# Attention plus MLP on one core: later planned DMA landings, packed output passes, sums by DMA

## The chip, the cores and the metric

One core of one Trainium2 chip runs the whole kernel. The metric is the device time of one execution in microseconds, the median of several runs. TensorE is called PE, VectorE DVE, ScalarE ACT, GpSimd POOL, and SyncE SP; SP here only issues DMAs.

## What is computed

The input x is 2048 tokens by 512 channels in bf16. It is normalised once; the result feeds attention with 32 heads of 16 channels and, normalised a second time, an MLP of width 1792. The output is x + attention + MLP.

```python
xn = layernorm(x)
q, k, v = split(xn @ wqkv)                     # 32 heads of 16
a = softmax(q @ k.T * 16 ** -0.5) @ v          # per head, 2048 x 2048 scores
h = gelu(layernorm(xn) @ w1 + b1)
out = x + a @ wo + h @ w2 + b2
```

## The kernel before

**Tiling.** The queries come in four query blocks of 512 tokens; in each, the 32 heads come in eight sets of four. A set of one block is the unit of the order: 32 sets, numbered g, `NS` = 8 per block. A set runs over 16 key tiles of 128 keys. For one key tile the four heads' scores are four matmuls, each on 32 rows of the array at its own row position (helper `qk`, L1033): 128 keys by 512 queries in a PSUM bank. Each such bank is a *unit*; 2048 units in all.

**Two ways to exponentiate.** A unit goes either to ACT, which takes two or three units in one instruction (L1216) and writes bf16 weights, or to DVE. On DVE a whole key tile of four units is made: each unit is evicted with a bias into int16 bits that read as float16 are a rough exponential (`build_dve`, L1305), and further terms come from adding constants to these integers (`dve_terms`): three terms by DVE in scratch buffers (L1327), the fourth by a DMA issued from POOL that adds a constant block `sdram` in place (L1339). Each term is multiplied with v separately, so a tile on DVE costs PE five passes where one on ACT costs one (helper `pv`, L1051; four matmuls of 32 columns a pass). PE accumulates one set's products in one PSUM bank, v's extra column of ones giving the softmax's sums. At most seven of 16 tiles of a set may go to DVE (`KD`); `next_d` starts one when fewer than `OPEN` are open, fewer than `OUT` are unfinished, an int16 buffer is free, and, within the running set, at least `RES` units are left. What DVE doesn't take goes to ACT.

**After a set** (`build_opost`): DVE copies the bank to `osb` (L1368). SP sends the four rows of sums to DRAM (L1370) and fetches them back as 128 by 16 values `lc` (L1372); DVE takes reciprocals (L1375); SP writes these out (L1377) and reads them back broadcast over partitions, `rlb` (L1380); DVE multiplies (L1382) into a slot of `ont`. POOL checks with four small instructions that the sums lie in the range for which the rough exponential holds (L1389 to L1395) and collects the answer; were it false, a slow version (`_general`) would run at the end. The last set does this with DVE transposes and no DRAM (`build_opost_last`).

**Output and MLP.** Once per block, `build_out` multiplies the eight sets with rows of wo that are padded to 32 rows a head with zeros (`wo_pad`), eight passes of four matmuls (helper `mm`, L597) per tile of 128 tokens. `build_mlp` and `build_down` do the MLP of a block: w1 is loaded in pieces through SP, the Gelu is two long ACT instructions (L1499). x plus b2 is made on POOL (L1515) from a loaded `x_r`, and DVE adds the MLP's product to it in `acc` (L1523), then the output product (L1545). `build_final` does the last two sets' part.

**The order.** `_Plan` lays out all instructions before the program is built. It is a list scheduler with the engines PE, ACT, DVE, POOL, SP and ACT's queue; each step has a duration, dependencies, a priority, and `lat`, the time after its end until a DMA's data is taken to have landed (for the accumulating DMA `SHL` = 6.0; for the four DMAs after a set 1.8, 2.4, 1.8 and 4.6). Each engine then executes its instructions strictly in the order that the plan found; semaphores make it wait where the data comes later than planned. Where the plan leaves PE idle while a set is open, it puts in matmuls on zeros (`fill`, L1622).

Of the kernel before, what the change touches and what calls it, by code (L numbers as in the profile page):

```python
# [22 lines left out]
P = 128  # L23
# [456 lines left out]
def kernel(  # L480
# [38 lines left out]
    NPU, NI, NTB, NON, NW1 = 15, 8, 4, 11, 4  # L519
# [5 lines left out]
    sdram = drp.tile([P, HS * QW], I16, name="sdram")  # L525
# [9 lines left out]
    b2_sb = const.tile([P, D], BF, name="b2_sb")  # L535
# [11 lines left out]
    wo_pad = const.tile([P, NB, 2, D], BF, name="wo_pad")  # L547
# [9 lines left out]
    x_r = const.tile([P, 2, D], BF, name="x_r")  # L557
# [14 lines left out]
    lc = const.tile([P, 2, LCW], F32, name="lc")  # L572
    rc = const.tile([P, 2, LCW], F32, name="rc")
    okt = const.tile([P, 2, LCW], F32, name="okt")
    okall = const.tile([P, LCW], F32, name="okall")
    ont = const.tile([P, NON, QW], BF, name="ont")
    ot = const.tile([P, 2, D], BF, name="ot")
# [26 lines left out]
    def pen(n):  # L604
        return 0.205 * n + 0.01
# [7 lines left out]
    def act(cols):  # L613
        return cols * 0.833e-3 + 0.07
# [26 lines left out]
    SHL = 6.0  # L641
    SLOT = 1.0
    PEND = _Op()
    OUT, OPEN, RES, RESL, SLK, ALP = 4, 2, 36, 28, 55.0, 0.0
# [6 lines left out]
    RATE, QO, PO, AO, DO = 22.75, 50.0, 44.5, 40.0, 14.5  # L651
# [56 lines left out]
    shc = ht[:, 0:HS, :].rearrange("p a q -> p (a q)").bitcast(I16)  # L708
    mk_sh = add("POOL", 2.2, lambda: I(nc.gpsimd.memset(shc, SHIFT[DMAT])), (), -60)
    ld_sh = dma("SP", sdram[:], shc, (mk_sh,), prio=-60, lat=6.0)  # L710
# [88 lines left out]
    ld_b2 = dma("SP", b2_sb[:], bass.AP(B_b2.tensor, B_b2.offset, [[0, P], [1, D]]), (ld_w2,), prio=62.0, lat=4.0)  # L799

    def c_wo(b):
        def fn():
            I(nc.vector.memset(wo_pad[:, b].rearrange("p e d -> p (e d)").bitcast(I32), 0))
        return fn
    mk_wo = [add("DVE", 0.55, c_wo(b), (xt_op[NT - 1],), 90.0, nb=90.0 + 5 * b) for b in range(NB)]
    wo_v = A_wo.rearrange("(b j e r) c -> j e r b c", b=NB, j=HS, e=2, r=DH)
    ld_wo = []
    for j in range(HS):
        for e in range(2):
            ld_wo.append(dma("SP", wo_pad[32 * j:32 * j + DH, :, e, :], wo_v[j, e],  # L810
                             deps=mk_wo, prio=110.0 + 3 * (2 * j + e), nb=110.0 + 3 * (2 * j + e)))
# [250 lines left out]
    d_busy = [0]  # L1062
# [13 lines left out]
    def next_d():  # L1076

        if len(todo) >= OPEN or d_busy[0] >= OUT or ib_free() is None:
            return
        g0 = max(stream["g"], 2)  # L1080
        for g in (0, 1, g0, g0 + 1):
            if g >= NG or not left_d[g]:
                continue
            if g < 2:
# [5 lines left out]
                d_busy[0] += 1  # L1090
# [13 lines left out]
            d_busy[0] += 1  # L1104
# [14 lines left out]
    def attach(i, d, fits, after, key, pool):  # L1119
# [4 lines left out]
        rider[i] = (g, k, j, pool, op)  # L1124
# [3 lines left out]
        if not js:  # L1128
            todo.remove(d)

    def ride(i, us):
        rows = {x[2] for x in us}
        key = ("d", i)
        pool = early if i < NU2 // 2 else misc

        def f(_, take=False, give=None):
            if not take:
                return 0.0
            next_d()
            for d in todo:  # L1140
                fits = [j for j in d[2] if j not in rows]
                if fits:
                    free = room(pool, key)
                    if free is not None and free <= I.now + 0.05:
                        attach(i, d, fits, us[-1][2] + 1, key, pool)
                    break
            return None
        return f

    def rides(i):  # L1150
        g, k, j, pool, op = rider[i]
        qk(pool.bank(("d", i)), g, k, j)
        I.more.append(op)


    def ride_alone(x):
        key = ("d", ("alone", x))
# [83 lines left out]
    def build_pv(g):  # L1241
# [11 lines left out]
        o = add("PE", pen(len(ks)), fpv, list(dict.fromkeys(deps)), pr - PO, acq=((o_ready, g),),  # L1253
# [60 lines left out]
    def dve_terms(g, k, sl, ins, dl):  # L1314
# [5 lines left out]
        uses, adds, first_o = [], [], None  # L1320
        for t in range(1, TERMS):
            if t < DMAT:
# [12 lines left out]
            else:  # L1335

                def f3():
                    d_busy[0] -= 1
# [334 lines left out]
```

## Time and profile before

| | |
|---|---|
| time, median of 3 runs | 876.03 us (875.35 to 878.42) |
| the profiled execution | 877.58 us |
| its span, first to last instruction | 875.7 us |
| mean granted TensorE clock | 0.943 |
| DMA moved in the span | 92.10 MB, mean 105 GB/s |

The span is the profile's own; the execution's time has about 1.9 us around it. Busy time counts instructions of the engines themselves, not DMA issues on SP. An idle time is put down to what ended it. The granted clock is 1.00 at 2.4 GHz and 0.50 at 1.2 GHz.

### The profile page before, as it was taken

What the parts mean: (1) busy time and instruction counts of PE and PEld (TensorE: products, weight loads), DVE (VectorE), ACT (ScalarE), POOL (GpSimd) and SP (SyncE); (2) the same over time, 40 slices, a digit from 0 to 9 for tenths busy, and PEclk for the clock granted to TensorE, in tenths of its full rate; (3) what the DMA queues carried; (4) which work ended last, traced back from release to release, by engine and by line L of the source; (5) the groups of instructions that cost most, each with busy time, mean ns of one, the idle gap of its engine ahead of it and who ended that gap; (6) DMA issues with size and microseconds to landing.
All of it is one profiled execution on the core that took longest, in us unless ns stands there. A gap on an engine that the chain in (4) does not pass through costs nothing. (4 is left out here: it accounts for less than half of the span.)

```text
span 875.7 us, 23298 instructions
## 1 busy us (share of the span) xinstructions
PE 803.3 (92%) x9823; PEld 255.1 (29%) x9824; DVE 716.4 (82%) x1219; ACT 768.5 (88%) x665; POOL 201.2 (23%) x294
## 2 busy tenths in 40 slices
PE   8999798989999899899998999899989999999996
PEld 3432232223332232223322223223322233232332
DVE  8869698867798888788988887787787999789873
ACT  6889699887999899969988899897988999999993
POOL 2201222204222112222212221212222233113211
PEclk9999799978999999969998899989997999999999
DMA  6311678533666656535657557535473767646634
GB/s 205 105 25 24 113 131 133 96 57 72 105 130 114 119 108 136 99 64 108 115 91 138 102 115 132 104 74 98 74 135 62 136 126 141 142 80 104 119 74 99
DMA packets 72509, 92.10 MB, mean 105 GB/s; under 512 B 42580, under 2 KB 52692, under 8 KB 72400
## 3 DMA queue, kind: packets, MB, share of 16 engines
q0 software_dynamic: 17424, 63.45, 42.6%
q1 hardware_dynamic: 53104, 25.68, 11.5%
q8 instruction: 78, 1.28, 0.6%
q10 hardware_dynamic: 1872, 1.44, 0.5%
q14 instruction: 31, 0.25, 0.1%
HBM read 87.42 MB, written 3.13 MB: 103 GB/s over the span
## 5 line engine op out<-in xcount | busy, mean ns | idle before, releaser
L1216 ACT ACTIVATE p_sb<-ps 128x1536 bf16<-128x1536 f32 (+1 forms) x638 | 727.0, 1233 | 85.2 <-PE ps L1033 72.4
L1033 PE MATMUL ps<-qz,kt 32*128 32x512 bf16 x2048 | 315.9, 394 | 26.8 <-DVE it L1305 9.7
L1305 DVE TENSOR_SCALAR it<-ps 128x512 int16<-128x512 f32 x244 | 162.3, 680 | 25.0 <-PE ps L1033 24.6
L1051 PE MATMUL ps<-it,va 128*32 128x512 f16 x1940 | 161.2, 396 | 19.3 <-DVE it L1327 10.5
L1305 DVE TENSOR_SCALAR x_sb<-ps 128x512 int16<-128x512 f32 x240 | 157.8, 680 | 15.8 <-PE ps L1033 15.5
L1033 PEld LDWEIGHTS <-kt 32*128 32x128 bf16 x2048 | 80.7, 91 | 288.3 <-issue 279.1
L1051 PE MATMUL ps<-p_sb,va 128*32 128x512 bf16 x1564 | 158.5, 401 | 2.0 <-DVE ot L1545 0.8
L1051 PEld LDWEIGHTS <-va 128*32 128x32 bf16 x3984 | 87.2, 96 | 197.3 <-issue 174.3
L1327 DVE TENSOR_SCALAR it<-x_sb 128x2048 int16<-128x2048 int16 x180 | 122.7, 696 | 6.6 <-PE ps L1051 6.0
L1327 DVE TENSOR_SCALAR it<-it 128x2048 int16<-128x2048 int16 x183 | 124.7, 700 | 3.2 <-PE ps L1051 2.4
L1339 POOL DMA_DIRECT2D x_sb<-sdram x60 | 63.2, 1054 | 231.1 <-PE ps L1051 137.9
L1339 POOL DMA_DIRECT2D it<-sdram x61 | 65.0, 1067 | 220.1 <-PE ps L1051 110.7
L597 PE MATMUL ps<-yT,w_r 128*32 128x512 bf16 x896 | 59.3, 385 | 4.1 <-DVE x_sb L1305 1.8
L597 PE MATMUL ps<-w_sb,ht 128*32 128x512 bf16 x896 | 59.4, 385 | 0.5 <-DVE it L1305 0.4
L1051 PE MATMUL ps<-x_sb,va 128*32 128x512 f16 x480 | 49.2, 408 | 5.2 <-DMA x_sb<-sdram 5.2
L1489 DVE TENSOR_SCALAR ht<-ps,b_sb 128x512 bf16<-128x512 f32 x56 | 41.7, 744 | 12.7 <-PE ps L597 12.6
L1389 POOL TENSOR_SCALAR okt<-lc 128x16 f32<-128x16 f32 x31 | 17.4, 562 | 115.6 <-DMA lc<-ldram 115.6
L1622 PE MATMUL ps<-ones_bf,zeros_bf 128*32 128x512 bf16 x432 | 43.8, 459 | 0.0
L1382 DVE TENSOR_TENSOR ont<-osb,rlb 128x512 bf16<-128x512 f32 x31 | 21.2, 684 | 20.1 <-DMA rlb<-rdram 20.1
L597 PE MATMUL ps<-wo_pad,ont 128*32 128x512 bf16 x512 | 34.4, 386 | 3.2 <-DVE it L1305 1.8
L1515 POOL TENSOR_TENSOR wkv<-x_r,b_sb 128x512 f32<-128x512 bf16 x16 | 20.0, 1258 | 60.6 <-DMA x_r<-in_A_x_dram 35.3
L597 PEld LDWEIGHTS <-w_r 128*32 128x32 bf16 x896 | 23.2, 96 | 27.0 <-issue 11.9
(95 smaller groups left out, 374.7 us busy)
## 6 DMA issues: line engine op xcount, KB each, us to landing
it<-sdram POOLq DMA_DIRECT2D x61, 512.0 KB, 6.3
x_sb<-sdram POOLq DMA_DIRECT2D x60, 512.0 KB, 5.9
rlb<-rdram SPq DMA_DIRECT2D x31, 256.0 KB
w_r<-in_B_w_dram SPq DMA_DIRECT2D x56, 128.0 KB
x_r<-in_A_x_dram SPq DMA_DIRECT2D x16, 128.0 KB
w_sb<-in_B_w_dram SPq DMA_DIRECT2D x1, 1792.0 KB
out_dram<-ot SPq DMA_DIRECT2D x12, 128.0 KB
x_sb<-in_A_x_dram SPq DMA_DIRECT2D x2, 512.0 KB
```

Of the source, the lines that this page charges most:

```text
L597: I(nc.tensor.matmul(dst[32 * j:32 * j + 32], lhsT=lhsT[:, 32 * j:32 * j + 32], rhs=rhs, start=start, stop=stop, tile_position=(0, 32 * j)))
L1033: I(nc.tensor.matmul(ps[:, bank, :], lhsT=kt[lo:lo + 32, s // 2, k * P:(k + 1) * P], rhs=qz[lo:lo + 32, (qt * NB + s // 2) % NQB, s % 2, : ...
L1051: I(nc.tensor.matmul(ps[32 * j:32 * j + 32, o_bank[g], :], lhsT=vals[:, h * VS:h * VS + 32], rhs=wts(j), start=pv_done[g] == 1, stop=end, ...
L1216: I(nc.scalar.activation(p_sb[:, s0:s1, :].rearrange("p a b -> p (a b)"), ps[:, b0:b0 + n, :].rearrange("p a b -> p (a b)"), AF.Exp, scale ...
L1305: I(nc.vector.tensor_scalar(out=ib[sl][:, j, :], in0=ps[:, pool.bank(key), :], scalar1=LEVEL, scalar2=0.0, op0=ALU.add, op1=ALU.max))
L1327: I(nc.vector.tensor_scalar(out=tb[x].rearrange("p j q -> p (j q)"), in0=ib[sl].rearrange("p j q -> p (j q)"), scalar1=float(SHIFT[t]), sc ...
L1339: I(nc.gpsimd.dma_start(out=ib[sl].rearrange("p j q -> p (j q)"), in_=sdram[:], accum_op=ALU.add))
L1382: e4 = add("DVE", dve(QW), lambda: I(nc.vector.tensor_tensor(out=ont[:, slot, :], in0=osb[:, i2, :], in1=rlb[:], op=ALU.mult)), [e3] + lis ...
L1389: I(nc.gpsimd.tensor_scalar(out=okt[:, 0, :], in0=lc[:, i2, :], scalar1=L_MIN, scalar2=None, op0=ALU.is_ge))
L1489: I(nc.vector.tensor_scalar(out=ht[:, fc, :], in0=ps[:, misc.bank(key), :], scalar1=b1_sb[:, fc:fc + 1], scalar2=None, op0=ALU.add))
L1515: xb_ = add("POOL", 0.8, lambda c=c, qi=qi: I(nc.gpsimd.tensor_tensor(out=acc[:, c, :], in0=x_r[:, qi % 2, :], in1=b2_sb[:], op=ALU.add)), ...
L1622: I(nc.tensor.matmul(ps[32 * j:32 * j + 32, o_bank[opened], :], lhsT=zeros_bf[:, 0:32], rhs=ones_bf[:], start=False, stop=False, tile_posi ...
```

## The change

In the planner: longer landing times for the accumulating DMA (6.0 to 8.0, its issue 1.0 to 1.1) and for the DMAs after a set; a limit of four unfinished DVE tiles (`OUT`) falls away, `RES` and `RESL` rise, `RATE`, the assumed time of a set, falls; the planned overhead of an ACT instruction falls by 15 ns, that of one kind of eviction rises by 60 ns. Some new knobs (`RIDE`, `WAITO`) are at values that change nothing.

In the program:
- An even set's product goes into `ont` as before; an odd set's goes into `ons`, and four SP DMAs move its 16 rows per head into the 16 rows of `ont` that the even set leaves unused. `ont` has seven slots of two sets each. The output multiplies two sets at once with wo as it is (`wo_r`). Only the last two sets use padded rows (`wo_l`).
- x plus b2 is made by two POOL DMAs: one that converts x to f32 into `acc`, one that adds b2, read with a zero step over the partitions.
- The range check is made once per query block over the sums of all its sets; `lc` keeps all sets' sums.
- In the last set the fourth term is also made by DVE.
- Gone are `x_r`, `b2_sb`, `wo_pad` with its four DVE memsets and eight loads.

```diff
-    NPU, NI, NTB, NON, NW1 = 15, 8, 4, 11, 4
+    NPU, NI, NTB, NON, NW1 = 15, 8, 4, 7, 4
...
-        return cols * 0.833e-3 + 0.07
+        return cols * 0.8333e-3 + AOV
...
-    SHL = 6.0
+    AOV, RIDE, WAITO = 0.055, 1, 0
+    SHL, XL = 8.0, 5.0
+    L1, L2, L3, LM = 2.3, 3.4, 6.5, 3.0
...
-    OUT, OPEN, RES, RESL, SLK, ALP = 4, 2, 36, 28, 55.0, 0.0
+    OPEN, RES, RESL, SLK, ALP = 2, 50, 42, 55.0, 0.0
...
-    RATE, QO, PO, AO, DO = 22.75, 50.0, 44.5, 40.0, 14.5
+    RATE, QO, PO, AO, DO = 21.75, 50.0, 44.5, 40.0, 14.5
...
+    mk_wo = add("POOL", 0.8, lambda: I(nc.gpsimd.memset(wo_l[:], 0.0)), (), -50)
+    ld_wo = [dma("SP", wo_r[:], A_wo.rearrange("(b p) c -> p b c", p=P), (ld_w2,), prio=110.0, nb=110.0,
+                 lat=6.0)]
...
-        if len(todo) >= OPEN or d_busy[0] >= OUT or ib_free() is None:
+        if len(todo) >= OPEN or ib_free() is None:
...
+        dmat = DMAT if g < NG - 1 else TERMS
         for t in range(1, TERMS):
-            if t < DMAT:
+            if t < dmat:
...
-                a = add("POOL", 1.0, f3, adds + [first_o, ld_sh], dl + t - AO - F2, lat=SHL)
+                a = add("POOL", 1.1, f3, adds + [first_o, ld_sh[t]], dl + t - AO - F2, lat=SHL)
...
-        slot = g % NON
+        i2, odd = g % 2, g % 2
+        slot = g // 2 % NON
+        dst = ons[:, g // 2 % 2, :] if odd else ont[:, slot, :]
...
-                 [e0] + before, pr - 500, lat=1.8)
+                 [e0] + before, pr - 500, lat=L1)
...
-            pr - 500, lat=2.4)
+            pr - 500, lat=L2)
...
-            pr - 500, lat=1.8)
+            pr - 500, lat=L1)
...
-                 [e3, last_rlb[0]], pr - 500, lat=4.6)
+                 [e3, last_rlb[0]], pr - 500, lat=L3)
...
+        if odd:
+            on_op[g] = ons_use[g // 2] = [add("SP", 0.45, lambda j=j: I(nc.sync.dma_start(
+                ont[32 * j + DH:32 * j + 32, slot, :], ons[32 * j:32 * j + DH, g // 2 % 2, :])),
+                [e4] + on_op[g - 1], pr, lat=LM) for j in range(HS)]
...
+        if g % NS == NS - 1 or g == NG - 2:
+            check_l(g // NS, g % NS + 1, pr)
...
+            v, ok = lc[:, qt * NS:qt * NS + n, :], okt[:, :, 0:n, :]
+            I(nc.gpsimd.tensor_scalar(out=ok[:, 0], in0=v, scalar1=L_MIN, scalar2=None, op0=ALU.is_ge))
+            I(nc.gpsimd.tensor_scalar(out=ok[:, 1], in0=v, scalar1=L_MAX, scalar2=None, op0=ALU.is_le))
+            I(nc.gpsimd.tensor_tensor(out=ok[:, 0], in0=ok[:, 0], in1=ok[:, 1], op=ALU.mult))
+            I(nc.gpsimd.tensor_tensor(out=okall[:, 0:n, :], in0=okall[:, 0:n, :], in1=ok[:, 0],
                                       op=ALU.mult))
...
-            xr = dma("SP", x_r[:, qi % 2, :], x2[qi * P:(qi + 1) * P, :],
-                     list(x_use.get(qi - 2, ())), pr - 10, nb=pr - 20)
...
-            xb_ = add("POOL", 0.8, lambda c=c, qi=qi: I(nc.gpsimd.tensor_tensor(
-                out=acc[:, c, :], in0=x_r[:, qi % 2, :], in1=b2_sb[:], op=ALU.add)),
-                [xr, ld_b2] + wait, pr - 5)
+            xb_ = add("POOL", 1.0, lambda c=c, qi=qi: I(nc.gpsimd.dma_start(
+                out=acc[:, c, :], in_=x2[qi * P:(qi + 1) * P, :])), wait, pr - 30, lat=XL)
+            xb_ = add("POOL", 1.0, lambda c=c: I(nc.gpsimd.dma_start(
+                out=acc[:, c, :], in_=b2_all, accum_op=ALU.add)), (xb_,), pr - 20, lat=XL)
...
-            steps = [(ont[:, g % NON, cs], wo_pad[:, (g % NS) // 2, g % 2, :]) for g in gs]
+            steps = [(ont[:, (qt * NB + b) % NON, cs], wo_r[:, b, :]) for b in bs]
```

## Rows read from the trace of the kernel before

**Rows 1.** The page, part 1: busy us, share of the span, instructions
```profile
PE 803.3 (92%) x9823; PEld 255.1 (29%) x9824; DVE 716.4 (82%) x1219; ACT 768.5 (88%) x665; POOL 201.2 (23%) x294
```

**Rows 2.** The waits of all engines: us in total, times, longest us
```profile
ACT p_sb L1216 <- PE ps L1033: 72.4, 79, 7.0
DVE rc L1375 <- DMA lc<-ldram: 20.9, 12, 6.5
DVE ont L1382 <- DMA rlb<-rdram: 20.1, 11, 3.0
POOL okt L1389 <- DMA lc<-ldram: 115.6, 26, 16.4
```

**Rows 3.** Groups by line: shapes, count | busy us, mean ns | idle before
```profile
L1216 ACT ACTIVATE p_sb<-ps 128x1536 bf16<-128x1536 f32 (+1 forms) x638 | 727.0, 1233 | 85.2 <-PE ps L1033 72.4 <-PE ps L1051 8.7 <-ACT p_sb L1216 0.4
L1305 DVE TENSOR_SCALAR it<-ps 128x512 int16<-128x512 f32 x244 | 162.3, 680 | 25.0 <-PE ps L1033 24.6
L1327 DVE TENSOR_SCALAR it<-it 128x2048 int16<-128x2048 int16 x183 | 124.7, 700 | 3.2 <-PE ps L1051 2.4
L1339 POOL DMA_DIRECT2D it<-sdram x61 | 65.0, 1067 | 220.1 <-PE ps L1051 110.7 <-PE ps L1033 85.6 <-DVE it L1327 10.4
L1339 POOL DMA_DIRECT2D x_sb<-sdram x60 | 63.2, 1054 | 231.1 <-PE ps L1051 137.9 <-PE ps L1033 74.5 <-DVE it L1327 6.8
L1515 POOL TENSOR_TENSOR wkv<-x_r,b_sb 128x512 f32<-128x512 bf16 x16 | 20.0, 1258 | 60.6 <-DMA x_r<-in_A_x_dram 35.3 <-PE ps L597 23.0 <-DVE ont L1382 2.3
L597 PE MATMUL ps<-wo_pad,ont 128*32 128x512 bf16 x512 | 34.4, 386 | 3.2 <-DVE it L1305 1.8 <-DVE ont L1418 1.2 <-DVE r2b L1467 0.2
```

**Rows 4.** Timeline, 84 to 98 us: start, us, instruction, idle before, releaser
```profile
94.79 0.25 DVE L1375 RECIPROCAL rc<-lc 128x16 f32<-128x16 f32 x1 [6.50 <-DMA lc<-ldram]
95.64 0.62 PE L1051 MATMUL ps<-it,va 128*32 128x512 f16 x4 [6.47 <-DVE it L1327]
96.91 1.45 ACT L1216 ACTIVATE p_sb<-ps 128x1536 bf16<-128x1536 f32 x1 [6.68 <-PE ps L1033]
```

**Rows 5.** Windows, the twelve low-clock stretches: length, busy us, PEclk, DMA, GB/s
```profile
90.20:100.40 10.20, 4.76 (x38) 1.07 (x37) 4.49 (x8) 2.50 (x3) 4.00 (x6) 0.50 0.30 55
185.80:202.80 17.00, 16.20 (x108) 3.69 (x111) 8.62 (x13) 9.52 (x6) 2.26 (x2) 0.50 0.03 9
271.10:274.50 3.40, 3.40 (x30) 0.73 (x22) 3.05 (x5) 2.41 (x2) 0.76 (x1) 0.50 0.42 80
370.10:387.20 17.10, 17.10 (x116) 3.52 (x119) 12.21 (x19) 9.87 (x8) 0.88 (x1) 0.50 0.21 38
585.10:595.40 10.30, 10.03 (x57) 2.68 (x60) 9.70 (x18) 8.23 (x5) 1.83 (x5) 0.50 0.12 10
sum 95.50, PE 87.66 PEld 19.37 DVE 67.03 ACT 55.66 POOL 17.55; mean PE 7.31 PEld 1.61 DVE 5.59 ACT 4.64 POOL 1.46
```

**Rows 6.** Windows, six stretches from 90.1, 152, 296, 475, 497 and 656 together
```profile
sum 46.80, PE 34.76 PEld 8.10 DVE 33.65 ACT 20.82 POOL 13.09; mean PE 5.79 PEld 1.35 DVE 5.61 ACT 3.47 POOL 2.18
```

**Rows 7.** Timeline before two low-clock stretches beside the Gelu
```profile
183.48 0.69 DVE L1382 TENSOR_TENSOR ont<-osb,rlb 128x512 bf16<-128x512 f32 x1 [2.53 <-DMA rlb<-rdram]
369.62 0.40 PE L1051 MATMUL ps<-it,va 128*32 128x512 f16 x4 [2.32 <-DMA it<-sdram]
```

**Rows 8.** The tile sdram, the accumulating DMAs: who waited for it, issue to landing
```profile
  PE ps L1051: 13.3, 17
DMA to landing us min/median/max: 5.2/5.9/9.1
```

**Rows 9.** Timeline of 466 to 476 us: one broadcast's issue and its reader
```profile
467.15 0.54 SPq L1380 DMA_DIRECT2D rlb<-rdram  x1
475.50 0.69 DVE L1382 TENSOR_TENSOR ont<-osb,rlb 128x512 bf16<-128x512 f32 x1 [2.99 <-DMA rlb<-rdram]
```

**Rows 10.** Windows, 280 to 304, 490 to 514 and 700 to 728 together
```profile
sum 76.00, PE 69.81 PEld 22.30 DVE 69.36 ACT 69.41 POOL 19.81; mean PE 23.27 PEld 7.43 DVE 23.12 ACT 23.14 POOL 6.60
```

**Rows 11.** Timeline of the end
```profile
867.29 0.59 ACT L1586 CAST yT<-ps 128x512 bf16<-128x512 f32 x1 [6.98 <-PE ps L597]
```

## What the change will do to the time

> **What bounds the kernel now.** I read the page's busy line first, then the waits, the timeline around the largest pauses, and last the stretches in which TensorE's granted clock is low. The busy line says who could bound: PE 92%, ACT 88%, DVE 82%, POOL 23% [rows 1]. PE's share is inflated by filler matmuls and by time at half clock, so I go by ACT. In undisturbed stretches ACT runs without a break; its softmax exponentials take 727.0 us in 638 instructions and leave 85.2 us idle before them, 72.4 us of it waiting for the score matmuls of L1033 [rows 2, 3]. Span is ACT's work plus these holes, so the question is what makes PE late.
>
> The reader is to see one pattern. DVE takes its work in a fixed order, and in that order stand the two steps of each set that need a round trip through DRAM: the reciprocal (L1375) and the multiplication (L1382). At 88 to 97 us the reciprocal waits 6.50 us for its sums, PE then waits 6.47 us for the DVE step queued behind it, and ACT 6.68 us for PE [rows 4]. Over the run DVE waits 20.9 us in 12 places for the sums and 20.1 us in 11 for the broadcast reciprocals [rows 2], 41.0 us in all. The second half of the damage is the clock: twelve stretches ahead of the tail run at the lower level of 1.2 GHz, granted 0.50, 95.5 us together, and ACT is busy in only 55.7 us of them [rows 5]. The first of them, 10.2 us with ACT busy 2.5, begins at 90.2, inside that pause. Six stretches around such DVE waits last 46.8 us with ACT busy 20.8: 26.0 us lost [rows 6]. Three more low-clock stretches lie beside the Gelu, from 185.8, 370.1 and 585.1: just before the first DVE had waited 2.53 us for reciprocals, before the second PE had waited 2.32 us for an accumulating DMA [rows 7], and the third is like the first. ACT loses 7.5, 7.2 and 2.1 us in these [rows 5]. That makes 42.8 us, half of the 85.2, that begin with a DMA landing later than the written order assumed.
>
> **The change part by part.**
>
> *Longer latencies in the planner.* They are no instructions; they move DVE, PE, POOL and SP steps later in the fixed orders. An accumulating DMA lands 5.2 to 9.1 us after issue, median 5.9 [rows 8]; the plan assumed 1.0 + 6.0 and now assumes 1.1 + 8.0 = 9.1, as late as the latest. So the 13.3 us that PE waits for these [rows 8] should nearly go. The hop to the sums is planned 0.5 + 1.0 us later in its two DMAs, the broadcast 0.5 + 1.9 us; one broadcast was issued at 467.15 and let its reader go at 475.50, 8.35 us later [rows 9], against 5.1 planned before and 7.0 now. So a wait can shrink by what the plan adds, but need not end. Taking 1.5 us off each of 12 waits and 1.9 off each of 11 removes at most 38.9 of the 41.0 us; the longest, 6.5, keeps 5.0, and those already under 1.5 give only what they have. I estimate that 29 of 41 go, 71%. Of the 42.8 us of ACT time I take 60%, less than 71%, since a shorter pause can still cost the clock: **−26 us**. Ends: 0 (each wait is replaced) and −42.8. What is late next: score matmuls waiting for DVE evictions, as in the low-clock stretch at 271.1 [rows 5], which none of these waits begins.
>
> The later order has a price. Each DVE-made tile (four evictions, L1305, three adds, L1327, one accumulating DMA) holds its int16 buffer and its set's PSUM accumulator 2.1 us longer in the plan, and the threshold after which no such tile is started in the running set rises from 36 to 50 units. The nearest row is the wait of 2.32 us behind one such DMA; I put **+2 us**, ends −13 and +41 (both worked out under the rivals).
>
> *Two sets packed into one output pass.* Before, every set's output pass used 16 of each 32 rows: 512 matmuls, 128 passes of four. Now 12 token tiles take 4 passes, the last 4 take 3 + 2: 68. So 60 go. The 128 took 34.4 us of PE [rows 3], 0.27 each, some of them at half clock: 60 are 16.1 us of PE. What of it lies on the path? In three stretches that hold such passes ACT is busy 69.4 of 76.0 us [rows 10], so 6.6 us could be gained there, and two of the six stretches of [rows 6] lie in them (from 296 and 497), counted already. I take **−2 us**, ends 0 and −16.1; the rest becomes filler.
>
> Added for it: after each odd set up to 29 four SP DMAs of 16 rows, 60 issues. At the 0.54 us of an SP issue [rows 9] that is 32 us of a queue that mostly waits. But they wait for the odd set's multiplication, and queued behind them are the next set's sum DMAs and the loads of w1. Cover: ont is needed only in the next query block's first quarter. Without it the price is one round trip per block, about 7 us three times; I take 0. The padded copy of wo goes (four DVE memsets near 100 us become one on POOL), eight loads become nine, on SP at a time when nothing needs them: 0.
>
> *x plus bias by DMA.* Removed: 16 SP loads and 16 POOL additions of 1258 ns [rows 3]. Added: 32 POOL issues. As the accumulating ones take 1067 ns [rows 3], that is 34 us for 20 us, on an engine 77% idle. The pair's second DMA waits for the first, and behind it on POOL stand the accumulating DMAs of DVE's tiles, for which PE waits. Planned landing 1.0 + 5.0, the same kind's median 5.9: the queue is held by 0 to 3.1 us, 16 times. Their cover is the 9.1 us now planned for landings of median 5.9. I take 0; ends 0 and +16 (a third of 49.6 reaching PE). PE's down passes do not read the sum, only DVE's addition does.
>
> *One range check per query block.* 31 groups of four small POOL instructions become four larger ones. POOL's 115.6 us of waiting for the sums [rows 2] goes, and with it what stood behind on POOL. POOL is off the path: 0 beyond the DMA waits counted.
>
> *Last set.* Its tiles get a fourth DVE add (700 ns, [rows 3]) in place of the DMA. In the tail the last exponential ends at 860.3 and ACT next works at 867.3, after 6.98 us [rows 11]; between lie late tile passes, three output passes that go (0.8 us), and a landing. I take **−2 us**, ends +2 and −5.
>
> **The sum.** −26 + 2 − 2 − 2 = −28 us. The profiled execution took 877.58 us (span 875.7 and 1.9 around it), 1.55 above the median of the runs shown; 877.6 − 28 = 849.6 there, on the scale of the median 876.0 − 28 = **848 us**.
>
> **Rivals.** (A) *More work moves to DVE.* The 29 us that DVE no longer waits are worth 29 / 4.8 = 6 tiles (4 × 0.68 + 3 × 0.70 us). A tile takes four units off ACT, 727.0/1564 = 0.465 us each, 1.86 in all: −11 us, and a little more from the output passes, −13; with the main sum 848 − 15 = 833 us when the +2 goes too. For: DVE and PE both gain room. Against: the longer hold of buffers and the raised threshold. Chance 0.14.
>
> (B) *The clock still falls.* Most low stretches follow such a wait, of 2 to 6.5 us in [rows 4, 7], but three of the twelve, the one at 271.1 among them [rows 5], follow none of these waits. If only half of the twelve go, at 39.8/12 = 3.3 us of ACT each, the gain is 20 us, less 5 for the later plan: 861 us. Thinner output stretches would help this to happen. The Trainium skill, "TensorE: Matmul & The Clock Gate", section "HAM oscillation", says that pauses between bursts send the array back to its lower clock, so that the next burst starts cold; by that rule taking passes away is no clean gain. The trace agrees in that a pause comes first [rows 4, 5]; no row shows fewer passes doing it. Chance 0.14.
>
> (C) *Nothing measurable.* The waits on DRAM are replaced by waits for evictions of tiles that are now all behind schedule at once, or the change's order does not hold its latencies because DMAs of x, bias and ont slow the small ones: 876 us. Chance 0.09.
>
> (D) *Slower: fewer tiles on DVE.* Buffers and accumulators held longer, and tiles started for the next set that cannot be accumulated until its accumulator opens, fill the eight int16 buffers; then no new tile is started and ACT takes its units. There are 121 such tiles (61 + 60, [rows 3]). Each lost one costs 1.86 us of ACT, so at 15 lost the 28 us are gone; at 22 lost the time is 876 + 13 = 889 us. For: ACT has no slack to take them. Against: 121 over 30 sets is four per set, against seven allowed and eight buffers. Chance 0.11.
>
> **The numbers.** The forecast keeps 0.52, by its own bounds 838 to 860. Faster is forecast, A and B: 0.80; within 0.5% (871.6 to 880.4, about what measurement can tell from no change): C, 0.09; slower: D, 0.11. The range takes in A and B and reaches towards C: 829 to 871, leaving C, D and the outer edge of A outside.
>
> **What would show it.** Right: DVE's waits for lc and rlb fall to about 12 us, PE's for accumulating DMAs below 4; low-clock time falls from 95 us to under 45; ACT's idle before exponentials from 85 to about 57; ont passes count 272 matmuls; accumulating issues stay at 115 to 125 without the bias ones. Wrong: under 106 tiles on DVE (D), six or more low-clock stretches (B), DVE's waits unchanged or moved to L1305 (C), POOL's issues waiting on their own landings with PE behind them.

## The result and the profile after

The changed kernel takes 840.6 us, median of 4 runs (831.6 to 844.0), against 876.5 for the kernel before in runs beside it: ratio 0.957, 95% interval 0.949 to 0.966. The forecast was 848 in a range of 829 to 871. The profiled execution took 843.7 us with a span of 841.9 and a mean granted clock of 0.970 (before 0.943).

The busy line of the page after (us, share of the span, instructions), to be held against [rows 1]:

```profile
PE 779.8 (93%) x9595; PEld 253.3 (30%) x9596; DVE 699.5 (83%) x1199; ACT 767.2 (91%) x670; POOL 172.0 (20%) x195
```

ACT's busy time is 767.2 us where it was 768.5: no work went off the engine that bounds. So nearly all of the 33.8 us that the span lost must have been idle time. The groups by line of the changed kernel, in the columns of [rows 3]:

```profile
L1220 ACT ACTIVATE p_sb<-ps 128x1024 bf16<-128x1024 f32 (+1 forms) x643 | 726.0, 1256 | 54.0 <-PE ps L1036 43.9 <-PE ps L1054 7.5 <-ACT p_sb L1220 0.2
L1314 DVE TENSOR_SCALAR it<-ps 128x512 int16<-128x512 f32 x240 | 158.5, 681 | 15.2 <-PE ps L1036 14.4
L1314 DVE TENSOR_SCALAR x_sb<-ps 128x512 int16<-128x512 f32 x232 | 152.6, 680 | 15.6 <-PE ps L1036 14.9
L1348 POOL DMA_DIRECT2D it<-sdram x57 | 59.2, 1039 | 288.3 <-PE ps L1054 115.7
L1348 POOL DMA_DIRECT2D x_sb<-sdram x56 | 60.7, 1085 | 203.8 <-PE ps L1054 92.4
L1538 POOL DMA_DIRECT2D wkv<-in_B_b_dram x16 | 18.4, 1323 | 23.2 <-DMA wkv<-in_A_x_dram 17.5 <-DVE it L1314 2.5 <-DVE ont L1394 1.6
L597 PE MATMUL ps<-wo_r,ont 128*32 128x512 bf16 x240 | 16.7, 396 | 0.2 <-DVE it L1314 0.2
```

The exponentials (now L1220) take 726.0 us as before, and their idle time falls from 85.2 [rows 3] to 54.0: 31.2 of the 33.8 us stand in this one row. The output passes have 240 matmuls here and 16 + 16 with `wo_l` in the end, 272 for 512. The filler matmuls rose from 432 to 492, which is 1.3 us more of PE. Accumulating issues are 57 + 56 = 113, and DVE makes (240 + 232) / 4 = 118 tiles for 121.

The waits after, in the columns of [rows 2] (L1387 is the reciprocal, L1394 the multiplication, in odd sets into `ons`):

```profile
ACT p_sb L1220 <- PE ps L1036: 43.9, 34, 8.0
POOL okt L1414 <- DMA lc<-ldram: 37.0, 4, 18.9
DVE rc L1387 <- DMA lc<-ldram: 17.7, 11, 5.6
POOL wkv L1538 <- DMA wkv<-in_A_x_dram: 17.5, 6, 5.8
DVE ont L1394 <- DMA rlb<-rdram: 10.8, 3, 6.3
DVE ons L1394 <- DMA rlb<-rdram: 10.1, 3, 6.3
```

And the tile `sdram`, who waited for the accumulating DMAs and how long they took, beside [rows 8]:

```profile
  PE ps L1054: 0.2, 1
DMA to landing us min/median/max: 5.3/6.5/10.7
```

PE waits 0.2 us for accumulating DMAs where it waited 13.3. DVE's waits for its two trips through DRAM, however, are 17.7 + 10.8 + 10.1 = 38.6 us; they were 41.0. They stand in 17 places instead of 23 and the three longest hold 18 us of them.

The windows of three of the four longest low-clock stretches (the fourth, from 678.8, also lasts 6.8 us), and the sum over all seven that lie ahead of the tail, in the columns of [rows 5]:

```profile
173.60:190.70 17.10, 14.23 (x95) 3.61 (x98) 12.02 (x19) 10.12 (x6) 0.58 (x1) 0.50 0.04 7
211.20:218.00 6.80, 5.16 (x39) 1.20 (x38) 2.73 (x5) 1.62 (x2) 0.00 (x0) 0.50 0.05 12
282.90:289.70 6.80, 4.30 (x38) 1.14 (x40) 4.34 (x8) 1.75 (x2) 0.00 (x0) 0.50 0.61 124
...
sum 47.70, PE 40.17 PEld 9.77 DVE 31.63 ACT 24.30 POOL 3.23; mean PE 5.74 PEld 1.40 DVE 4.52 ACT 3.47 POOL 0.46
```

Time at the granted 0.50 is halved, from 95.5 to 47.7 us, and ACT's idle time inside it falls from 39.8 to 47.7 − 24.3 = 23.4. What is left follows the pattern of before. The timeline around these three stretches, and two writes of the sums to DRAM further on (start, us, instruction, idle before and its releaser):

```profile
164.80 0.58 SPq L1392 DMA_DIRECT2D rlb<-rdram  x1
164.83 0.88 POOL L1348 DMA_DIRECT2D x_sb<-sdram  x1 [6.25 <-PE ps L1054]
166.73 0.87 POOL L1348 DMA_DIRECT2D it<-sdram  x1 [1.02 <-PE ps L1036]
...
174.78 0.69 DVE L1394 TENSOR_TENSOR ont<-osb,rlb 128x512 bf16<-128x512 f32 x1 [6.27 <-DMA rlb<-rdram]
...
176.13 1.90 PE L597 MATMUL ps<-xnT,wkv 128*32 128x512 bf16 x16 [4.20 <-DVE it L1314]
...
211.50 0.69 DVE L1394 TENSOR_TENSOR ons<-osb,rlb 128x512 bf16<-128x512 f32 x1 [6.32 <-DMA rlb<-rdram]
...
284.52 0.25 DVE L1387 RECIPROCAL rc<-lc 128x16 f32<-128x16 f32 x1 [5.56 <-DMA lc<-ldram]
...
287.95 2.37 ACT L1220 ACTIVATE p_sb<-ps 128x1536 bf16<-128x1536 f32 x2 [5.91 <-PE ps L1036]
...
374.54 0.53 SPq L1382 DMA_DIRECT2D ldram<-osb  x1
375.39 1.03 POOL L1348 DMA_DIRECT2D it<-sdram  x1 [15.22 <-PE ps L1054]
376.26 0.32 SPq L1384 DMA_DIRECT2D lc<-ldram  x1
...
445.41 1.38 POOL L1348 DMA_DIRECT2D it<-sdram  x1 [0.42 <-PE ps L1036]
448.41 1.38 POOL L1348 DMA_DIRECT2D it<-sdram  x1 [1.62 <-PE ps L1054]
449.12 0.54 SPq L1382 DMA_DIRECT2D ldram<-osb  x1
453.02 0.34 SPq L1384 DMA_DIRECT2D lc<-ldram  x1
```

A broadcast is issued at 164.80, and two accumulating DMAs are issued beside it. Its reader starts at 174.78, 10.0 us after the issue, where the plan now has 0.5 + 6.5. DVE had stood 6.27 us, PE stands 4.20 behind it, and the clock is at 0.50 from 173.6 to 190.7. The rows from 374.54 on show where the hops are late: SP issues the read-back (L1384) once the write of the sums (L1382) has landed. With an accumulating DMA issued 0.85 us after the write, that is 1.72 us after the write's issue (374.54 to 376.26); with two issued 3.7 and 0.7 us ahead of the write, it is 3.90 (449.12 to 453.02).

### The profile page after: what moved, and what is told of

Read it like the earlier page. It is cut to its first block, busy times and chain, and to the rows that moved or that the text cites. A ratio compares the mean times of both kernels' runs of the same rounds, so it can differ in the third digit from the quotient of the medians.

```text
span 841.9 us, 22838 instructions
## 1 busy us (share of the span) xinstructions
PE 779.8 (93%) x9595; PEld 253.3 (30%) x9596; DVE 699.5 (83%) x1199; ACT 767.2 (91%) x670; POOL 172.0 (20%) x195
## 4 chain that ended last, share of the span: by engine, by line
PE 39%; ACT 19%; DMA 18%; DVE 15%; issue 9%; SPq 0%; DVEq 0%; ACTq 0%
ACT p_sb L1220 18%; PE ps L1054 14%; PE ps L1036 12%; PE ps L597 11%; DMA lc<-ldram 5%; DMA rlb<-rdram 5%; DMA ldram<-osb 4%; DMA rdram<-rc 3%; DVE it L1337 3%; DVE x_sb L1314 3%; DVE it L1314 2%; ACT ht L1522 1%; PE ps L1641 1%; DVE stats L731 1%; DVE osb L1380 1%
## 5 line engine op out<-in xcount | busy, mean ns | idle before, releaser
L1220 ACT ACTIVATE p_sb<-ps 128x1024 bf16<-128x1024 f32 (+1 forms) x643 | 726.0, 1256 | 54.0 <-PE ps L1036 43.9
L1036 PEld LDWEIGHTS <-kt 32*128 32x128 bf16 x2048 | 86.6, 91 | 291.4 <-issue 285.7
L1314 DVE TENSOR_SCALAR x_sb<-ps 128x512 int16<-128x512 f32 x232 | 152.6, 680 | 15.6 <-PE ps L1036 14.9
L1054 PE MATMUL ps<-it,va 128*32 128x512 f16 x1904 | 153.4, 390 | 2.0 <-DVE it L1337 1.6
L1337 DVE TENSOR_SCALAR it<-x_sb 128x2048 int16<-128x2048 int16 x176 | 115.7, 682 | 5.4 <-PE ps L1054 4.9
L1348 POOL DMA_DIRECT2D it<-sdram x57 | 59.2, 1039 | 288.3 <-PE ps L1054 115.7
L597 PEld LDWEIGHTS <-ht 128*32 128x32 bf16 x896 | 21.9, 97 | 23.1 <-issue 7.8
L1536 POOL DMA_DIRECT2D wkv<-in_A_x_dram x16 | 12.0, 752 | 74.1 <-DVE ot L1566 51.9
L1522 ACT ACTIVATE ht<-ht 128x3584 bf16<-128x3584 bf16 x8 | 25.1, 3182 | 0.0
L1544 DVE TENSOR_TENSOR wkv<-ps,wkv 128x512 f32<-128x512 f32 x16 | 11.0, 688 | 16.5 <-PE ps L597 16.3
```

Of the source, the lines that this page charges most:

```text
L597: I(nc.tensor.matmul(dst[32 * j:32 * j + 32], lhsT=lhsT[:, 32 * j:32 * j + 32], rhs=rhs, start=start, stop=stop, tile_position=(0, 32 * j)))
L1036: I(nc.tensor.matmul(ps[:, bank, :], lhsT=kt[lo:lo + 32, s // 2, k * P:(k + 1) * P], rhs=qz[lo:lo + 32, (qt * NB + s // 2) % NQB, s % 2, : ...
L1054: I(nc.tensor.matmul(ps[32 * j:32 * j + 32, o_bank[g], :], lhsT=vals[:, h * VS:h * VS + 32], rhs=wts(j), start=pv_done[g] == 1, stop=end, ...
L1220: I(nc.scalar.activation(p_sb[:, s0:s1, :].rearrange("p a b -> p (a b)"), ps[:, b0:b0 + n, :].rearrange("p a b -> p (a b)"), AF.Exp, scale ...
L1314: I(nc.vector.tensor_scalar(out=ib[sl][:, j, :], in0=ps[:, pool.bank(key), :], scalar1=LEVEL, scalar2=0.0, op0=ALU.add, op1=ALU.max))
L1337: I(nc.vector.tensor_scalar(out=tb[x].rearrange("p j q -> p (j q)"), in0=ib[sl].rearrange("p j q -> p (j q)"), scalar1=float(SHIFT[t]), sc ...
```

## The experiments

The theory under test is the prediction's: the gain is the planned landing times, since a DMA later than planned stops an engine that works in a fixed order, and the rest of the change gives next to nothing. The rivals are that the program's parts (packing, sums by DMA, one check per block) earn a share, or that any other order would do as well. Each ratio is against the kernel before in runs on the same chip, whose time lay between 876 and 886 us; so ratios are compared, not times.

### The two kinds of landing time, alone in the kernel before

`e1` takes only the accumulating DMA's times:

```diff
-    SHL = 6.0
+    SHL = 8.0
...
-                a = add("POOL", 1.0, f3, adds + [first_o, ld_sh], dl + t - AO - F2, lat=SHL)
+                a = add("POOL", 1.1, f3, adds + [first_o, ld_sh], dl + t - AO - F2, lat=SHL)
```

> The kernel before with the accumulating DMA planned 8.0 instead of 6.0 us to landing (issue 1.1 for 1.0) and nothing else. Theory A (late accumulating DMAs set the time, through PE's pauses and the clock): PE's 13.3 us of waiting for them fall below 2, low-clock time falls from 95 to under 60 us, the time is 850 to 865 us. Theory B (the trips through DRAM after each set are what counts, as the prediction had it): PE's waits for accumulating DMAs go, but the time stays at 870 to 880. Theory C (the output passes made the gain): 872 to 880.

Measured: ratio 0.988 (0.982 to 0.993). PE's waits for accumulating DMAs fall from 13.3 to 2.5 us, DVE's waits rise from 41.0 to 47.6, and ACT's idle time before exponentials goes from 85.2 to 69.8. The gain is about 11 us, at the border between the two expectations; the low-clock time ahead of the tail is 61 us, just missing theory A's mark of under 60. The accumulating DMAs are then a part of the cause and not all of it. The gain is clear of the noise of runs, but no larger than what another order alone can do (`e10` below).

`e2` takes only the times of the four DMAs after a set:

```diff
-                 [e0] + before, pr - 500, lat=1.8)
+                 [e0] + before, pr - 500, lat=2.3)
...
-            pr - 500, lat=2.4)
+            pr - 500, lat=3.4)
...
-            pr - 500, lat=1.8)
+            pr - 500, lat=2.3)
...
-                 [e3, last_rlb[0]], pr - 500, lat=4.6)
+                 [e3, last_rlb[0]], pr - 500, lat=6.5)
```

> The kernel before with the four DMAs after a set planned 2.3, 3.4, 2.3 and 6.5 us to landing (for 1.8, 2.4, 1.8, 4.6) and nothing else. Theory B: DVE's 41.0 us of waiting for lc and rlb fall to 10 to 15, the time is 850 to 858 us. Theory A: DVE's waits stay above 25 us and the time is 865 to 880. Theory C: 872 to 880.

Measured: ratio 0.981 (0.975 to 0.987). DVE's waits fall to 30.4 us: those for the sums from 20.9 to 5.4, while those for the broadcast rise from 20.1 to 25.0. PE's waits for accumulating DMAs grow to 20.9, and ACT's idle time is 70.0. The gain, about 17 us, is smaller than theory B had it, and DVE's waits and the time are where theory A expected them. A part of the gain may have been handed on to the other late DMA, for which PE now waits 7.6 us more.

### The two kinds taken back, in the changed kernel

`e3` sets the accumulating DMA back, its issue from 1.1 to 1.0 too:

```diff
-    SHL, XL = 8.0, 5.0
+    SHL, XL = 6.0, 5.0
```

> The changed kernel with the accumulating DMA planned 6.0 us to landing again (issue 1.0). Theory A: PE waits 10 us or more for these DMAs, low-clock time rises from 48 us to over 70, the time is 852 to 868 us. Theory B: 836 to 846 as it was. Theory C: 836 to 846.

Measured: ratio 0.974 (0.966 to 0.982), 1.8% above the changed kernel's 0.957. The execution profiled was the fastest of its runs, 844.8 us for a median of 855.3; in it PE waits 8.1 us in 12 places for accumulating DMAs, where it waited 0.2. That execution was within 2 us of the changed kernel's profiled one, and ACT's idle time in it is 52.9 us for 54.0: these waits cost nothing there that the profile shows, and where the slower runs of `e3` lost their time is not known. The marks of theory A in the profile, 10 us of waiting and over 70 us at low clock, did not appear: the low-clock time ahead of the tail is 48 us, as in the changed kernel.

`e4` sets the four DMAs after a set back:

```diff
-    L1, L2, L3, LM = 2.3, 3.4, 6.5, 3.0
+    L1, L2, L3, LM = 1.8, 2.4, 4.6, 3.0
```

> The changed kernel with the four DMAs after a set planned 1.8, 2.4, 1.8 and 4.6 us to landing again. Theory B: DVE's waits rise from 38.6 us to over 60 and the time is 855 to 870 us. Theory A: 836 to 850. Theory C: 836 to 846.

Measured: 883.3 us, ratio 1.007 (1.002 to 1.011). With all the rest of the change in place, the whole gain is gone, and a little more, past the 855 to 870 us that theory B expected. The waits of this run:

```profile
ACT p_sb L1220 <- PE ps L1036: 75.3, 52, 8.1
DVE rc L1387 <- DMA lc<-ldram: 30.4, 13, 4.9
DVE ont L1394 <- DMA rlb<-rdram: 19.9, 5, 8.1
DVE ons L1394 <- DMA rlb<-rdram: 13.6, 4, 6.7
```

DVE waits 63.9 us for its trips, the most of any run, and ACT's wait for score matmuls is back at 75.3, where [rows 2] had 72.4. So the packed passes, the DMAs for x and bias and the single check do not make the kernel faster by themselves.

### The planner's numbers for DMAs and sets, none of the program

`e5` is the kernel before with the edits of `e1` and `e2` and the change's thresholds and set time (`OUT` at 99 is no limit):

```diff
-    OUT, OPEN, RES, RESL, SLK, ALP = 4, 2, 36, 28, 55.0, 0.0
+    OUT, OPEN, RES, RESL, SLK, ALP = 99, 2, 50, 42, 55.0, 0.0
...
-    RATE, QO, PO, AO, DO = 22.75, 50.0, 44.5, 40.0, 14.5
+    RATE, QO, PO, AO, DO = 21.75, 50.0, 44.5, 40.0, 14.5
```

> The kernel before with every number of the planner that the change moves for DMAs and sets (both landing times, no limit of unfinished tiles, thresholds 50 and 42, set time 21.75), and the program's instructions as before. Theory D (the gain is in the planned latencies together; packing, the sums by DMA and the check add little): 845 to 858 us beside 876 to 880. Theory E (the latencies give about 10 to 15 us each as in the two runs alone, the rest is what the program no longer does): 858 to 870. Theory C (output passes): 868 to 880.

Measured: ratio 0.969 (0.961 to 0.977), the product of `e1` and `e2` (0.988 × 0.981 = 0.969). Three quarters of the change's 4.3% come with numbers of the planner alone. The interval touches that of the whole change (0.949 to 0.966), so what remains is between nothing and some 2%. It falls to the program and to two numbers that no run changed by themselves, the planned overheads of an ACT instruction and of one kind of eviction.

### The program's parts, each undone in the changed kernel

`e6` undoes the packing: `wo_pad` and its loads are back, `ont` has a slot for each of 11 sets, no copies of odd sets.

```diff
-            steps = [(ont[:, (qt * NB + b) % NON, cs], wo_r[:, b, :]) for b in bs]
+            steps = [(ont[:, g % NON, cs], wo_pad[:, (g % NS) // 2, g % 2, :]) for g in gs]
```

> The changed kernel with the output made set by set again: padded wo, eleven slots of ont, 128 passes, no copies of odd sets. Theory C: 855 to 870 us beside 876 to 880, score matmuls late in the output stretches. Theory D: 838 to 850. Prediction's term: 2 us more than the changed kernel, ends 0 and 16.

Measured: 835.3 us, ratio 0.958 (0.950 to 0.966), that of the changed kernel (0.957). Halving the output passes gives nothing that can be measured; with intervals of 0.8% to either side, a few us could not be.

`e7` undoes the sums by DMA:

```diff
-            xb_ = add("POOL", 1.0, lambda c=c, qi=qi: I(nc.gpsimd.dma_start(
-                out=acc[:, c, :], in_=x2[qi * P:(qi + 1) * P, :])), wait, pr - 30, lat=XL)
-            xb_ = add("POOL", 1.0, lambda c=c: I(nc.gpsimd.dma_start(
-                out=acc[:, c, :], in_=b2_all, accum_op=ALU.add)), (xb_,), pr - 20, lat=XL)
+            xr = dma("SP", x_r[:, qi % 2, :], x2[qi * P:(qi + 1) * P, :],
+                     list(x_use.get(qi - 2, ())), pr - 10, nb=pr - 20)
+            xb_ = add("POOL", 0.8, lambda c=c, qi=qi: I(nc.gpsimd.tensor_tensor(
+                out=acc[:, c, :], in0=x_r[:, qi % 2, :], in1=b2_sb[:], op=ALU.add)),
+                [xr, ld_b2] + wait, pr - 5)
```

> The changed kernel with x plus bias made as before: x loaded by SP, the sum on POOL. Prediction's term 0, ends 0 and 16 us in favour of this run: 836 to 846 us. Theory F (the two POOL DMAs crowd the DMAs after a set): DVE's waits for lc and rlb fall from 38.6 to under 28 us and the time is 822 to 834. Theory E: 846 to 856, because the loads return to SP.

Measured: 842.5 us, ratio 0.959 (0.948 to 0.969): no difference that intervals of 1% to either side can tell.

`e8` makes the check once per set again:

```diff
-        if g % NS == NS - 1 or g == NG - 2:
-            check_l(g // NS, g % NS + 1, pr)
+        check_l(g, 1, pr)
```

> The changed kernel with the range check after each set, four small instructions as before. Theory G (POOL's wait for the sums held up accumulating DMAs): POOL waits over 100 us for lc again, PE waits over 5 us for accumulating DMAs, 848 to 860 us. Prediction's term 0: 836 to 846.

Measured: 846.9 us, ratio 0.965 (0.956 to 0.974). The interval overlaps that of the changed kernel, so no price is shown, and one of 1 to 2% is not excluded. In the profiled execution, the slowest of the four (861.6 us), POOL waits 155.6 us in 27 places for the sums, for 37.0 in 4, and PE waits 0.5 us for accumulating DMAs, not the 5 of theory G.

### The planner's other numbers

`e9` puts the thresholds and the set time back in the changed kernel:

```diff
-    OPEN, RES, RESL, SLK, ALP = 2, 50, 42, 55.0, 0.0
+    OPEN, RES, RESL, SLK, ALP = 2, 36, 28, 55.0, 0.0
...
-    RATE, QO, PO, AO, DO = 21.75, 50.0, 44.5, 40.0, 14.5
+    RATE, QO, PO, AO, DO = 22.75, 50.0, 44.5, 40.0, 14.5
```

> The changed kernel with the planner's thresholds and set time as before (36 and 28 units, 22.75), its landing times kept. Theory D' (landing times alone carry the gain): 836 to 848 us. Theory H (starting fewer DVE tiles late in a set is what lets a set end on time): 855 to 868, more ACT idle in front of each set's end.

`e10` is a control that changes only the set time, to a value that means nothing, for the same work in another order:

```diff
-    RATE, QO, PO, AO, DO = 21.75, 50.0, 44.5, 40.0, 14.5
+    RATE, QO, PO, AO, DO = 21.5, 50.0, 44.5, 40.0, 14.5
```

> A control: the changed kernel with the planner's set time at 21.5 for 21.75, which changes priorities a little and nothing else, so another order of the same work. All theories: the changed kernel's time within 1%, 833 to 849 us; how far it is off says what a difference of one order from another is worth.

Measured: `e9` 842.2 us, ratio 0.950 (0.940 to 0.959); `e10` 837.4 us, ratio 0.945 (0.939 to 0.950). They lie 0.8 and 1.3% below the changed kernel's ratio. In `e9` DVE makes 110 tiles and the exponentials take 737.5 us, 11 more, but their idle time is 36.8, 17 less: one nearly pays for the other. The control was expected within 1%, and its ratio is a little outside; DVE's waits are 31.6 us in it for 38.6. The changed kernel was not run again in that session, so 1.3% holds what the order alone moves together with the difference of two sessions. A difference of about 1% between two orders, as in `e1`, `e6`, `e7`, `e8` and between `e5` and the whole change, can thus not be put down to what was edited. The whole change (4.3%), `e5` (3.1%) and `e4` against the changed kernel (5%) lie well beyond it, `e2` and `e3` (1.9 and 1.8%) in between.

### Longer still

If late trips are the cause, planning them later than the change does must go on gaining. `e11` and `e12` change one line of the changed kernel:

```diff
-    L1, L2, L3, LM = 2.3, 3.4, 6.5, 3.0
+    L1, L2, L3, LM = 3.5, 4.5, 8.0, 3.0
```

```diff
-    L1, L2, L3, LM = 2.3, 3.4, 6.5, 3.0
+    L1, L2, L3, LM = 4.5, 5.5, 10.0, 3.0
```

> The changed kernel with the four DMAs after a set planned 3.5, 4.5, 3.5 and 8.0 us to landing (for 2.3, 3.4, 2.3, 6.5), nearer to the hops beside accumulating DMAs in the traces. If DVE's waits still cost at 38.6 us (theory B as far as it is left): they fall below 20 and the time is 822 to 834. If what is left of them is off the path, or the later order gives it back in held accumulators: 836 to 850.

> The same with 4.5, 5.5, 4.5 and 10.0 us, at or above most hops measured. Theory B: DVE's waits below 8 us, 815 to 830. Rival: the output of a set comes so late in the plan, and the end so much later, that 10 us or more are given back: 838 to 855.

Measured: `e11` 830.1 us, ratio 0.938 (0.933 to 0.943); `e12` 816.0 us (814.2 to 818.6), ratio 0.922 (0.917 to 0.928). Both times are where theory B expected them. `e12` beats both kernels: it is 3.6% below the changed one by the ratios, and 2.4% below the control `e10` of the same session (`e11`: 2.0 and 0.7%). Its waits, its group of the exponentials, and its low-clock stretches:

```profile
ACT p_sb L1220 <- PE ps L1036: 8.4, 18, 2.7
DVE ont L1394 <- DMA rlb<-rdram: 6.0, 1, 6.0
DVE rc L1387 <- DMA lc<-ldram: 0.7, 3, 0.3
```

```profile
L1220 ACT ACTIVATE p_sb<-ps 128x1024 bf16<-128x1024 f32 (+1 forms) x640 | 720.4, 1259 | 18.8 <-PE ps L1036 8.4 <-PE ps L1054 7.9 <-ACT p_sb L1220 0.2
```

```profile
282.70:286.10 3.40, 3.40 (x31) 0.83 (x23) 2.04 (x5) 2.27 (x3) 1.33 (x2) 0.50 0.79 167
798.10:808.30 10.20, 2.92 (x30) 1.17 (x34) 1.82 (x4) 0.58 (x1) 0.00 (x0) 0.50 0.08 28
```

DVE's only long wait is in the tail, one low-clock stretch of 3.4 us is left ahead of it, and ACT's idle time before exponentials is 18.8 us. Its new cost is the end, in the timeline:

```profile
786.51 0.52 SPq L1382 DMA_DIRECT2D ldram<-osb  x1
788.21 0.32 SPq L1384 DMA_DIRECT2D lc<-ldram  x1
...
797.82 0.21 DVE L1387 RECIPROCAL rc<-lc 128x16 f32<-128x16 f32 x1
...
799.78 0.64 SPq L1392 DMA_DIRECT2D rlb<-rdram  x1
...
804.82 0.69 DVE L1394 TENSOR_TENSOR ont<-osb,rlb 128x512 bf16<-128x512 f32 x1 [5.99 <-DMA rlb<-rdram]
...
806.67 0.58 ACT L1605 CAST yT<-ps 128x512 bf16<-128x512 f32 x1 [19.50 <-PE ps L597]
```

The last exponential ends at 787.2 and the span at 814.0, 26.8 us later; after the change that was 14.1. The trip of the last set but one is planned with the long times too, and its reciprocal stands 9.6 us behind the read-back's issue without having waited for anything. Planning the last trip with shorter times was not tried.

### The runs side by side

Waits for late DMAs are DVE's for both trips and PE's for the accumulating DMAs, both from the views of waits. In `e3` and `e11` another 1.1 and 2.7 us before the same steps of DVE are put down to other DMAs and not counted. These columns and the clock come from the one profiled execution, the ratio from all runs; `e3` and `e5` were profiled in their fastest execution. `e8` is left out, as it was profiled in its slowest, 1.7% above its median.

| run | DVE's waits | PE's | together | ACT idle before exponentials | clock | ratio |
|---|---|---|---|---|---|---|
| before | 41.0 | 13.3 | 54.3 | 85.2 | 0.943 | 1 |
| e4, after, trips early | 63.9 | 0 | 63.9 | 86.2 | 0.942 | 1.007 |
| e1, before, accumulating later | 47.6 | 2.5 | 50.1 | 69.8 | 0.962 | 0.988 |
| e2, before, trips later | 30.4 | 20.9 | 51.3 | 70.0 | 0.964 | 0.981 |
| e3, after, accumulating early | 32.5 | 8.1 | 40.6 | 52.9 | 0.966 | 0.974 |
| e5, before, planner | 23.1 | 1.4 | 24.5 | 52.1 | 0.967 | 0.969 |
| e7, after, bias on POOL | 27.1 | 0.5 | 27.6 | 52.3 | 0.959 | 0.959 |
| e6, after, unpacked | 23.4 | 0 | 23.4 | 44.2 | 0.969 | 0.958 |
| after | 38.6 | 0.2 | 38.8 | 54.0 | 0.970 | 0.957 |
| e9, after, old thresholds | 29.5 | 0.5 | 30.0 | 36.8 | 0.987 | 0.950 |
| e10, after, control | 31.6 | 0 | 31.6 | 46.6 | 0.973 | 0.945 |
| e11, after, trips longer | 18.6 | 0 | 18.6 | 32.9 | 0.976 | 0.938 |
| e12, after, trips longest | 6.7 | 0 | 6.7 | 18.8 | 0.990 | 0.922 |

The two columns move together, with scatter: from the kernel before to `e12` the waits fall by 47.6 us and ACT's idle time by 66.4, 1.4 us of ACT for each us of waiting. More than one is what the pauses alone would not give; the stretches at half clock behind them are the likely rest, which no run separates from the pauses. The sum of waits does not order the middle of the table: `e5` has fewer than the changed kernel, about the same idle time, and a higher ratio.

## Why the prediction was right, and where not

**What bounds: right.** ACT's busy time did not move, and its idle time carried 31.2 of the 33.8 us. The cause named, DMAs that land later than the order assumed, is shown from both sides for the trips: `e4` takes their times back and loses everything, `e12` lengthens them and gains 2.4 to 3.6% more. For the accumulating DMAs it rests on `e1` and on PE's waits, which went.

**The term of the landing times (−26): right in the sum, wrong in its working.** ACT's idle time fell by 31.2 us under the whole change; `e5`, which holds this term and the price of the later order, gained 0.031 of the time, about 27 us, for −26 + 2 = −24. The step that failed is the one that took 29 of DVE's 41 us away: the profile shows 2.4. It subtracted what the plan adds from each old wait, as if every hop stayed where and as long as it was. But the change makes another order, in which other hops meet the accumulating DMAs, and the plan still lies below a hop that meets them: 0.5 + 2.3 us is planned for the write of the sums, whose median is 4.2 where such a DMA is ahead of it and in flight; 0.5 + 6.5 for the broadcast, which took 6.5 to 10.8 in the six places where its reader waited. In other orders of the changed kernel the waits are 23 to 33 us (`e3`, `e6`, `e7`, `e9`, `e10`), so 38.6 is a high draw; but the 12 us of the forecast appear only where the plan covers the loaded hop, between `e11` and `e12`. What seems to have made up for it is the other half of the same term, the accumulating DMAs. The prediction said that their 13.3 us should nearly go, and they did (0.2), but beyond one stretch gave them no size of their own; `e1` and the ratio of `e3` would put them at 1.2 and 1.8% of the time, against 1.9% for the trips in `e2` and 5% in `e4`, and neither of the first two lies far beyond what the control allows. That the sum came out so near is thus in part luck. The clock's share fell about as foreseen: low-clock time is 47.7 us and just misses the mark of under 45, ACT's idle time 54.0 where about 57 was.

The prediction also read too little into the accumulating DMAs of the kernel before. It takes the stretch from 271.1, and three of the twelve in all, to begin without any of these waits. PE, however, had just waited for an accumulating DMA ahead of that stretch, as it had for 1.30 us until 642.43, ahead of the one from 643.2:

```profile
270.30 0.40 PE L1051 MATMUL ps<-it,va 128*32 128x512 f16 x4 [1.11 <-DMA it<-sdram]
```

In the trace before, eleven of the twelve stretches begin during a wait of PE or DVE for a late DMA (1.1 to 6.5 us long) or at most 3.8 us after its end; in the trace after it is six of the seven ahead of the tail. The exception before is the stretch from 656.8, which the prediction had counted: its wait begins only at 664.9. Not every such wait brings a stretch; one of 3.57 us that ends at 396.1 after the change brings none.

**The price of the later order (+2): within its ends, not seen.** The longer hold is inside `e1` and `e2` and no run separates it; `e5` adds the thresholds and comes out at the product of the two, and `e9`, which takes the thresholds back, shows no sign of a price either way. Tiles on DVE fell by 3, not by 15.

**Packing (−2): not seen.** `e6` gives 0.958 for 0.957, which can't tell 2 us from nothing, but speaks against the end of −16. The 272 matmuls came as counted. That the rest becomes filler is not what the fillers show: their 1.3 us more of PE stand against some 14 us that the passes no longer take (34.4 to 16.7 + 3.2), and without packing `e6` has 472 of them, nearly as many.

**x plus bias (0): not contradicted.** `e7` shows no difference. POOL's queue was held by the pair for 17.5 us in 6 places, up to 5.8 at a time where 0 to 3.1 was worked out; the old form had waited 35.3 for x_r [rows 3], and PE's waits for accumulating DMAs, 0.2 us, show nothing held up behind it. The second DMA's landing is 6.7 us against 5.9 taken.

**Range check (0), last set (−2):** POOL's waits for sums fell from 115.6 to 37.0 us, and `e8` shows no clear price. From the last exponential to the end 14.1 us pass for 15.4 before: −1.3 for the −2.

**The rivals.** A (more tiles on DVE) did not happen: 118 for 121. D (fewer) neither. C's mark, DVE's waits unchanged, nearly did appear (38.6 for 41.0) while the time fell by 4.3%: the mark was a poor one, because it leaves out PE's waits for accumulating DMAs and because a sum of waits says nothing of how many of them begin a low-clock stretch. B's mark, six or more low-clock stretches, appeared as well (seven), at half the length; B's number of 861 did not come. B had leaned on the Trainium skill, "TensorE: Matmul & The Clock Gate", section "HAM oscillation", that pauses between bursts make the next burst start cold. The trace agrees: the three stretches shown above begin inside DVE's three longest waits (6.27, 6.32 and 5.56 us), and with the waits in `e12` all but one of the stretches ahead of the tail go too.

**What stays open.** Why `e4` is as bad as it is: from 0.957 and the 0.981 of `e2` one would expect 0.976, and it is 1.007. The trips' times are worth more in the changed kernel than in the kernel before; whether its added DMAs (x, bias, the copies into `ont`) lengthen the hops was not separated, since `e6` and `e7` each show shorter waits of DVE but the control does so too. The program's whole share, 0.957 against the 0.969 of `e5`, is at the edge of what these intervals tell.

## What to carry to other kernels

Where a written order holds landing times for DMAs, read the time from issue to release of the reader out of a trace of the whole kernel, with the other DMAs in flight, and plan at the long end of what is found: in these runs the trips planned longest cost, as far as is seen, only the tail, while a landing planned too early stopped an engine with everything queued behind it, and a stretch at half clock often followed. Such numbers of the planner should be swept before the program is touched; here three numbers in one line were worth another 2.4 to 3.6%, beside the 4.3% of the whole change; and a control that changes nothing of meaning should run beside them, since the order alone moved the ratio by up to 1.3%. In the tail, where nothing hides the distance, shorter ones may be better; no run here tried them.

## What the runs showed of the hardware

The small DMA's latency under load was not expected. The time from the issue of the 8 KB write of the sums to the issue of its read-back, which waits for its landing, has a median of 3.8 us in the kernel before (12 sets) and 4.2 after (13 sets, 1.7 to 8.2) where an accumulating DMA was issued ahead of the write and was in flight for most of that time; in the other sets the median is 1.7 in both. A 256 KB broadcast with a waiting reader came 5.0 us after its issue when alone (`e12`, 799.78 to 804.82) and 10.0 beside two accumulating DMAs (164.80 to 174.78). So the transfers were slower side by side, although different engines issue them. The Trainium skill says as much, "DMA: Bandwidth & Descriptors", section "Issuing engines are not separate DMA queues": DMAs of SP, ScalarE and GpSimd run on the same 16 engines and interleave. The trace agrees, with 1.72 against 3.90 us for the same transfer; where within the hop the 2.2 us arise no row here shows.
